# Two row buffers: taken from a pool for each batch, or made once and kept

## The chip, the cores and the metric

The kernel runs on one core of one Trainium2 chip. The metric is device time in microseconds for one execution; lower is better. Engines: TensorE (PE: matrix multiply, with PEld for its weight loads), VectorE (DVE), ScalarE (ACT), GpSimd (POOL) and SyncE (SP, which here issues most DMAs).

## The reference

Three parts follow one another, all in float32. `x` has 8 batches of 3072 tokens with 256 features.

1. The real part of a two-dimensional FFT of each batch (along tokens, then along features).
2. A mixture of 8 experts: every one of the 24,576 tokens is normalised, compared with 8 expert embeddings, sent to the best expert alone, and weighted by its softmax probability: `out[mask] = gate_w[mask, None] * (relu(x[mask] @ w1[e]) @ w2[e])`.
3. A gated layer on the result: `((x @ w_a) * (x @ w_b)) @ w_out`.

## The kernel before

The kernel has three stages that follow one another in one program: the batch stage (the transforms and the routing), the expert stage (groups of 256 tokens, sorted by expert), and the gated layer. In the trace the batch stage fills about the first 400 us. The program order of each engine is written out by hand (`manual_schedule`); nothing reorders it.

**One batch.** Batch `b` runs 8 steps `s1` (first half of the transform: 8 matmuls and 2 ScalarE copies each) and then 12 steps, `t` = 0 to 11. Each such step issues `s2(b, t)` (matmuls, one ScalarE copy `zs` at L378, two VectorE operations at L382) and then `s3(b, t - 2)`. `s3` makes two rows of 128 tokens: ScalarE copies one product out of PSUM (`qs`, L406), and VectorE writes row `t` (L407) and row 12 + `t` (L409) of the batch's row buffer `xo[b]`. So `s3(b, 0)` stands in the third step of the loop, and `s3(b, 10)` and `s3(b, 11)` stand in the first step of the next batch's `s1`. `post` then copies parts of the rows to their mirrored places (ScalarE, L421, for three values of `t` at a time).

**The row buffer.** `xo[b]` has 24 rows of 268 numbers on 128 partitions. There are two pools of one buffer each, `xo_p[0]` and `xo_p[1]`. Even batches take a tile from the first, odd batches from the second, at `t == 0` of `s3` (L389). The second pool is also used once at the start, as `spare` (L283), for small constants. A tile that is taken anew from a pool may be written when everything that used the pool's tile before it is over.

**Routing and scatters.** When a batch's rows are there, `route` (a chain of small VectorE operations, fed in between the other work by `advance`) finds the place of each token. Its last step (L557) makes `posi`, and then puts 24 scatters in `pool_q`: for `t` = 0 to 11, row `t` and row 12 + `t`. A scatter (L164) is an indirect DMA that GpSimd issues; it carries one row of 128 tokens from `xo[b]` to the sorted array `xs` in HBM. `drain(pool_q, ...)` issues one or two of them with each ScalarE copy that `mark` names, and `scatter` makes the scatter wait for that copy. The last ones of batch 6 are issued in one go behind the loop (L1024). In the program the scatters of batch `b` thus stand among the `s2` steps of batch `b + 1` and the `s1` steps of batch `b + 2`, whose rows go to the same buffer as those of `b`. GpSimd also does two of the folds of `x` for each batch (L257, `fold_v`).

**The end of the stage.** `p1b.close()` (L1026) gives back the pools on the right side, `xo_p[0]` among them, and the tiles of the expert stage (`slots[1]`, first written at L746) take their place. Rows of batch 7 stay in the other pool and are scattered during the expert stage.

Of the kernel before, what the change touches and what calls it, by code (L numbers as in the profile page):

```python
# [8 lines left out]
F32 = mybir.dt.float32  # L9
# [14 lines left out]
NT = 12  # L24
SEG = 67
ROW = 4 * SEG - 1
# [111 lines left out]
def moe_kernel(ctx, tc, x, emb, tau, w1, w2, wa, wb, wo, pa, pt, pr, nat, out):  # L138
# [44 lines left out]
    def scatter(idx_ap, src):  # L183
        i = spread(idx_ap, src, xs, NROWS - 1, "xs")
        if marks:
# [11 lines left out]
    xo_p = [p1b.enter_context(tc.tile_pool(name="xo0", bufs=1, side="right")),  # L197
            p1.enter_context(tc.tile_pool(name="xo1", bufs=1, side="left"))]
# [81 lines left out]
        return y  # L280


    spare = xo_p[1].tile([128, 2 * NT, ROW + 1], F32, name="xo").rearrange("p j c -> p (j c)")  # L283
    pcs = spare[:, 0:640]
    embt = spare[0:8, 640:896]
    su = ExitStack()
# [58 lines left out]
    xo = {}  # L345
# [40 lines left out]
    def s3(b, t):  # L386
        za, zb = zt.pop((b, t))
        if t == 0:
            xo[b] = xo_p[b % 2].tile([128, 2 * NT, ROW + 1], F32, name="xo")  # L389
            ssq[b] = r_p.tile([128, 2, NT], F32, name="ss", bufs=2)  # L390
        o = xo[b]
        ps = ps3.tile([128, 3, 137], F32, name="ps3")
        for i in range(2):
            q = 2 * t + i
            pe.matmul(ps[64 * i:64 * i + 64, 1, :], lhsT=tq(q), rhs=zb[:, i, :], start=True, stop=True)
        for i in range(2):
            q = 2 * t + i
            pe.matmul(ps[64 * i:64 * i + 64, 0, :], lhsT=tp(q), rhs=za[:, i, :], start=True, stop=True)
        pi = 0
        if t == 11:  # L400
            pi = 2
            for i in range(2):
                pe.matmul(ps[64 * i:64 * i + 64, 2, :], lhsT=tp2 if i else tp(22), rhs=za[:, i, :],
                          start=True, stop=True)
        qs = z_p.tile([128, 137], F32, name="qs")
        sc.copy(qs, ps[:, 1, :])  # L406
        ve.tensor_tensor(o[:, t, MAIN:MAIN + NCOL], ps[:, 0, :], qs, ALU.subtract)  # L407
        advance()
        ve.tensor_tensor(o[:, NT + t, MAIN:MAIN + NCOL], ps[:, pi, :], qs, ALU.add)  # L409
        advance()  # L410
# [157 lines left out]
    def advance(n=1):  # L568
        for _ in range(n):
            if routes:  # L570
                for g in list(routes):
                    r = next(g, 0)
                    if r == 0:
                        routes.remove(g)
                    if r != 1:
                        break
# [377 lines left out]
    for b in range(B):  # L954
# [3 lines left out]
        for s in range(8):  # L958
# [15 lines left out]
            if s == 0:  # L974
                s3(b - 1, 10)
                s3(b - 1, 11)
                post(b - 1, 9, 12)
                act_q.append(lambda b=b - 1, c=CHUNKS.get(b - 1, ((0, NT),))[-1]: start_route(b, *c))
# [23 lines left out]
        for t in range(NT + (2 if last else 0)):  # L1002
            if t < NT:
                s2(b, t)
            if t >= 2:
                s3(b, t - 2)
            if t in (5, 8, 11):
                post(b, t - 5, t - 2)
            if t == NT + 1:
                break  # L1010
            if t - 1 in chunks:
                act_q.append(lambda b=b, c=chunks[t - 1]: start_route(b, *c))
            if t % 3:
                drain(dve_q, 1)
            drain(act_q, 2)
            if last:
                advance(1)
                if t == 6:
                    weigh(0)
                if t == 8:  # L1020
                    turn(0)
# [237 lines left out]
    for st in range(NST):  # L1259
        G, p = divmod(st, NP)  # L1260
# [60 lines left out]
```

## Time and profile before

| | us |
|---|---|
| median of 3 runs (lowest, highest) | 3882.5 (3882.05, 3883.97) |
| the profiled execution's own time | 3879.51 |
| its span | 3877.7 |
| mean granted TensorE clock, share of full speed | 0.985 |

| engine | busy us | share of the span |
|---|---|---|
| PE | 3773.7 | 97% |
| DVE | 3121.0 | 80% |
| ACT | 1702.1 | 44% |
| POOL | 1136.6 | 29% |

The span is the time from the first to the last instruction of the profiled execution; its own time is 1.8 us more. Busy shares are means over three unlike stages. A stretch shows how busy each engine was between two times and which share of full speed TensorE's clock was granted (1.00 is 2.4 GHz, 0.50 is 1.2 GHz). In the lists in order of time a row is: start, duration, engine, line, operation, output and inputs, and in brackets how long the engine had been idle and what ended it; `issue` there means that no wait is seen. `DMA xs<-xo,posi` as a releaser is a scatter that has landed.

### The profile page before, as it was taken

Reading aid. Unit: us, or ns where it says so; the run is one execution under the profiler, and the core shown is the slowest. Engines: PE = TensorE matmul, PEld = TensorE weight load, DVE = VectorE, ACT = ScalarE, POOL = GpSimd, SP = SyncE. Lnnn points to the kernel's source line nnn. Section 1 sums busy time; section 2 is a strip of 40 time slices with the busy share of each in tenths; the row PEclk is TensorE's granted clock in tenths of the full one; section 3 lists DMA queues with packets and bytes.
Section 4 is the critical chain, followed back from the end, with each engine's and each line's share of the span. In section 5 each row is a group of like instructions: output and inputs, shape, how many; then the busy total and the mean of one; then the engine's idle time right before and its main releaser. Section 6 shows DMA issues by size and latency. Waiting matters only on the chain.

```text
span 3877.7 us, 68085 instructions
## 1 busy us (share of the span) xinstructions
PE 3773.7 (97%) x25556; PEld 3445.0 (89%) x25556; DVE 3121.0 (80%) x5097; ACT 1702.1 (44%) x3025; POOL 1136.6 (29%) x1017
## 2 busy tenths in 40 slices
PE   9888899999999999999999999999999999999998
PEld 8777899999999999888888888888888888888887
DVE  6766889899989987777788877788777788777886
ACT  4555566666666666433333333333333333333332
POOL 2666566667676643000000000000000000011011
PEclk8889899999999999999999999999999999999999
DMA  5444354333243231334334434444344344344331
GB/s 147 137 136 147 109 169 139 119 120 116 80 122 118 74 98 51 123 136 142 139 136 144 138 137 145 147 138 144 136 139 143 136 141 141 136 141 145 137 134 56
DMA packets 255048, 497.84 MB, mean 128 GB/s; under 512 B 151541, under 2 KB 184061, under 8 KB 245885
## 3 DMA queue, kind: packets, MB, share of 16 engines
q1 hardware_dynamic: 236284, 442.04, 35.1%
q0 software_dynamic: 18432, 51.44, 3.7%
q8 instruction: 201, 3.29, 0.3%
q14 instruction: 131, 1.07, 0.1%
HBM read 568.14 MB, written 95.14 MB: 171 GB/s over the span
## 4 chain that ended last, share of the span: by engine, by line
PE 59%; issue 18%; DVE 11%; POOL 2%; ACT 1%; DMA 0%; SPq 0%; POOLq 0%; ACTq 0%; DVEq 0%
PE pp L1142 7%; PE pp L1144 6%; PE pp L1143 6%; PE psy L819 5%; PE psy L820 5%; PE psy L821 5%; PE psh L794 5%; PE psh L790 5%; PE psh L792 4%; PE po L1212 3%; PE po L1210 3%; PE po L1211 3%; DVE big L1183 2%; DVE big L1168 2%; DVE gl L1194 1%
## 5 line engine op out<-in xcount | busy, mean ns | idle before, releaser
L164 POOL DMA_INDIRECT out_dram<-o,ig x192 | 215.3, 1121 | 2080.2 <-ACT o L1216 2033.5
L1189 ACT CAST gh<-big 128x512 fp32r<-128x512 f32 x576 | 355.8, 622 | 778.0 <-DVE big L1183 778.0
L1212 PE MATMUL po<-wo,gl 128*128 128x256 f32 x2304 | 651.1, 283 | 0.2 <-DVE gl L1194 0.2
L1210 PE MATMUL po<-wo,gh 128*128 128x256 f32 x2304 | 649.2, 282 | 1.6 <-ACT gh L1189 1.6
L1211 PE MATMUL po<-wo,gh 128*128 128x256 f32 x2304 | 647.4, 281 | 0.0
L747 DVE TENSOR_TENSOR s<-big,s 128x1024 fp32r<-128x1024 f32 x412 | 559.2, 1358 | 63.6 <-ACT s L746 62.2
L1142 PE MATMUL pp<-xo,slab 128*128 128x512 f32 x1440 | 582.8, 405 | 12.7 <-DVE big L1168 12.1
L1144 PE MATMUL pp<-xo,slab 128*128 128x512 f32 x1440 | 569.9, 396 | 0.0
L1143 PE MATMUL pp<-xo,slab 128*128 128x512 f32 x1440 | 566.7, 394 | 0.2 <-DVE xo L1126 0.2
L1211 PEld LDWEIGHTS po<-wo,gh 128*128 128x128 f32 x2304 | 435.5, 189 | 89.4
L1210 PEld LDWEIGHTS po<-wo,gh 128*128 128x128 f32 x2304 | 433.7, 188 | 88.9 <-ACT gh L1189 1.8
L819 PE MATMUL psy<-hh,s 128*128 128x256 f32 x1648 | 468.7, 284 | 13.5 <-ACT hh L802 13.5
L820 PE MATMUL psy<-hl,s 128*128 128x256 f32 x1648 | 468.4, 284 | 0.5 <-DVE hl L803 0.5
L821 PE MATMUL psy<-hh,s 128*128 128x256 f32 x1648 | 467.9, 284 | 0.0
L790 PE MATMUL psh<-xh,s 128*128 128x256 f32 x1648 | 452.9, 283 | 1.3 <-ACT xh L773 1.2
L794 PE MATMUL psh<-xh,s 128*128 128x256 f32 x1648 | 452.3, 283 | 0.0
L746 ACT CAST s<-big 128x1024 fp32r<-128x1024 f32 x412 | 428.8, 1041 | 16.4 <-DMA xs<-xo,posi 16.4
L1212 PEld LDWEIGHTS po<-wo,gl 128*128 128x128 f32 x2304 | 434.9, 189 | 0.4 <-DVE gl L1194 0.4
L1160 ACT COPY big<-pp 128x512 f32<-128x512 f32 x288 | 169.0, 587 | 584.7 <-PE pp L1144 581.9
L802 ACT ACTIVATE hh<-psh 128x512 fp32r<-128x512 f32 x412 | 246.4, 598 | 402.0 <-PE psh L794 271.1
L1194 DVE TENSOR_TENSOR gl<-big,gh 128x512 fp32r<-128x512 f32 x576 | 393.2, 683 | 2.9 <-ACT gh L1189 0.7
L1162 DVE TENSOR_TENSOR big<-pp,big 128x512 f32<-128x512 f32 x288 | 198.2, 688 | 238.2 <-PE pp L1144 209.5
(200 smaller groups left out, 8608.5 us busy)
## 6 DMA issues: line engine op xcount, KB each, us to landing
slab<-slabs SPq DMA_DIRECT2D x282, 896.0 KB
big<-in_w_dram SPq DMA_DIRECT2D x206, 1024.0 KB
big<-xs SPq DMA_DIRECT2D x103, 264.0 KB
ytd<-big SPq DMA_DIRECT2D x103, 256.0 KB
xr<-in_x_dram SPq DMA_DIRECT2D x32, 768.0 KB
big<-ytd SPq DMA_DIRECT2D x24, 1024.0 KB
slabs<-slab SPq DMA_DIRECT2D x12, 896.0 KB
xs<-xo,posi POOLq DMA_INDIRECT x192, 3.2
```

The lines of the kernel that those rows point to most:

```text
L747: ve.tensor_tensor(lo, r, hi.bitcast(F32), ALU.subtract)
L790: pe.matmul(ps[:, i, :], lhsT=wh, rhs=hi[:, k, :], start=(k == 0 and (u > 0 or i == 0)), stop=False, skip_group_check=True)
L794: pe.matmul(ps[:, i, :], lhsT=wl, rhs=hi[:, k, :], start=False, stop=last_, skip_group_check=True)
L819: pe.matmul(ps[:, c, :], lhsT=wh, rhs=a[:, i, :], start=st, stop=False, skip_group_check=True)
L820: pe.matmul(ps[:, c, :], lhsT=wh, rhs=l[:, i, :], start=False, stop=False, skip_group_check=True)
L821: pe.matmul(ps[:, c, :], lhsT=wl, rhs=a[:, i, :], start=False, stop=(f == 7), skip_group_check=True)
L1142: pe.matmul(ps, lhsT=t[:, wh, :], rhs=xh, start=start, stop=False, skip_group_check=True)
L1143: pe.matmul(ps, lhsT=t[:, wh, :], rhs=xl, start=False, stop=False, skip_group_check=True)
L1144: pe.matmul(ps, lhsT=t[:, wl, :], rhs=xh, start=False, stop=True, skip_group_check=True)
L1210: pe.matmul(ps, lhsT=ht, rhs=wos[0][:, f, :], start=(first_ and r % 2 == 0), stop=False, skip_group_check=True)
L1211: pe.matmul(ps, lhsT=ht, rhs=wos[1][:, f, :], start=False, stop=False, skip_group_check=True)
L1212: pe.matmul(ps, lhsT=lt, rhs=wos[0][:, f, :], start=False, stop=last_, skip_group_check=True)
```

## The change

The two row buffers are made once, before the loops, as the list `xos`. `s3` at `t == 0` no longer takes a tile: it names the one of the two that the batch uses. Buffers, sizes, places and all instructions stay as they are; lines behind the edit move by one.

```diff
-    spare = xo_p[1].tile([128, 2 * NT, ROW + 1], F32, name="xo").rearrange("p j c -> p (j c)")
+    xos = [p.tile([128, 2 * NT, ROW + 1], F32, name="xo") for p in xo_p]
+    spare = xos[1].rearrange("p j c -> p (j c)")
...
         if t == 0:
-            xo[b] = xo_p[b % 2].tile([128, 2 * NT, ROW + 1], F32, name="xo")
+            xo[b] = xos[b % 2]
```

The instructions of every engine stand in the same order before and after. What differs is which semaphores some of them wait for. This is VectorE at `s3(2, 0)` and `s3(2, 1)`, the first rows that are written to a used buffer; the instructions between are the routing of batch 1 (L538 to L549), a fold (L257) and `s2` (L382). `DMASW0` to `DMASW7` are the eight semaphores that the scatters count up in turn. Before:

```order
L407 TENSOR_TENSOR xo<-ps_1303,qs 128x137 [waits DMASW4_49,DMASW3_49,DMASW5_49,DMASW2_49,DMASW6_49,DMASW1_49,DMASW7_49,DMASW0_49,Activation_49]
L538 COPY xo<-natt 128x24
L409 TENSOR_TENSOR xo<-ps_1303,qs 128x137
L540 RECIPROCAL mx<-mx 128x24 [waits DVE_49]
L257 TENSOR_TENSOR big_71<-xr 96x4x127
L382 SCALAR_TENSOR_TENSOR zc<-sgnx,psb,psa 128x137 [waits PE_49,Activation_49]
L543 COPY xo<-mx 128x48 [waits DVE_49]
L543 COPY xo<-mx 128x48
L382 SCALAR_TENSOR_TENSOR zc<-sgnx,psb,psa 128x137
L547 TENSOR_TENSOR pref<-ps_122,prt 128x8
L407 TENSOR_TENSOR xo<-ps_1330,qs 128x137 [waits Activation_49]
L549 TENSOR_TENSOR inc<-inc,pref 128x192 [waits DVE_49]
```

And now, with all line numbers one higher:

```order
L408 TENSOR_TENSOR xo<-ps_1301,qs 128x137 [waits DMASW0_49,Activation_49]
L539 COPY xo<-natt 128x24
L410 TENSOR_TENSOR xo<-ps_1301,qs 128x137 [waits DMASW1_49]
L541 RECIPROCAL mx<-mx 128x24 [waits DVE_49]
L257 TENSOR_TENSOR big_71<-xr 96x4x127
L383 SCALAR_TENSOR_TENSOR zc<-sgnx,psb,psa 128x137 [waits PE_49,Activation_49]
L544 COPY xo<-mx 128x48 [waits DVE_49]
L544 COPY xo<-mx 128x48
L383 SCALAR_TENSOR_TENSOR zc<-sgnx,psb,psa 128x137
L548 TENSOR_TENSOR pref<-ps_122,prt 128x8
L408 TENSOR_TENSOR xo<-ps_1328,qs 128x137 [waits DMASW2_49,Activation_49]
L550 TENSOR_TENSOR inc<-inc,pref 128x192 [waits DVE_49]
```

The first L407 of the batch waited for all eight scatter semaphores and the others for none. Now each L407 and each L409 waits for one, that of the scatter that last read its row. This is so in each of batches 2 to 7: of the 96 L407, 6 had nine waits and 90 one; now 72 have two and 24 one, and 72 of the 96 L409 have one where none had any. On ScalarE the first L421 of each of these batches had nine waits; now 23 of L421 have seven (six scatter semaphores and VectorE's). On GpSimd one scatter waits for two loads into `spare` besides. Nothing else differs.

## Rows read from the trace of the kernel before

**Rows 1.** Waits, 0 to 1100 us: who waits for whom; us, times, longest

```profile
DVE xo L407 <- DMA xs<-xo,posi: 48.2, 6, 8.9
PE ps L395 <- DVE xo L409: 37.9, 6, 7.3
ACT s L746 <- DMA xs<-xo,posi: 16.4, 1, 16.4
```

**Rows 2.** VectorE in time order, L407 at t = 0

```profile
83.80 0.29 DVE L407 TENSOR_TENSOR xo<-ps,qs 128x137 f32<-128x137 f32 x1
129.71 0.30 DVE L407 TENSOR_TENSOR xo<-ps,qs 128x137 f32<-128x137 f32 x1 [8.75 <-DMA xs<-xo,posi]
176.71 0.30 DVE L407 TENSOR_TENSOR xo<-ps,qs 128x137 f32<-128x137 f32 x1 [8.76 <-DMA xs<-xo,posi]
319.67 0.30 DVE L407 TENSOR_TENSOR xo<-ps,qs 128x137 f32<-128x137 f32 x1 [8.02 <-DMA xs<-xo,posi]
364.70 0.30 DVE L407 TENSOR_TENSOR xo<-ps,qs 128x137 f32<-128x137 f32 x1 [4.99 <-DMA xs<-xo,posi]
```

**Rows 3.** VectorE in time order, L407 at t = 10, batches 1, 2, 6

```profile
101.97 0.30 DVE L407 TENSOR_TENSOR xo<-ps,qs 128x137 f32<-128x137 f32 x1 [2.21 <-ACT qs L406]
148.96 0.30 DVE L407 TENSOR_TENSOR xo<-ps,qs 128x137 f32<-128x137 f32 x1 [2.21 <-ACT qs L406]
339.50 0.30 DVE L407 TENSOR_TENSOR xo<-ps,qs 128x137 f32<-128x137 f32 x1 [2.06 <-ACT qs L406]
```

**Rows 4.** Stretches: length, busy us of PE, PEld, DVE, ACT, POOL, granted clock, DMA

```profile
84.00:90.00 6.00, 6.00 (x59) 4.79 (x57) 6.00 (x26) 3.11 (x10) 1.03 (x1) 1.00 0.36 93
224.00:230.00 6.00, 4.89 (x26) 3.91 (x27) 5.22 (x23) 1.05 (x5) 0.90 (x1) 0.50 0.46 120
```

**Rows 5.** GpSimd in time order, scatters of the steady batches

```profile
100.75 0.97 POOL L164 DMA_INDIRECT xs<-xo,posi  x1 [1.26 <-ACT yt L360]
127.13 0.97 POOL L164 DMA_INDIRECT xs<-xo,posi  x1 [0.30 <-issue]
134.72 0.97 POOL L164 DMA_INDIRECT xs<-xo,posi  x1 [6.61 <-issue]
210.90 1.14 POOL L164 DMA_INDIRECT xs<-xo,posi  x1 [0.30 <-issue]
212.35 1.21 POOL L164 DMA_INDIRECT xs<-xo,posi  x1 [0.31 <-issue]
```

**Rows 6.** GpSimd in time order, the last scatters of the batch stage

```profile
341.55 0.97 POOL L164 DMA_INDIRECT xs<-xo,posi  x1 [1.02 <-ACT yt L360]
369.71 0.97 POOL L164 DMA_INDIRECT xs<-xo,posi  x1 [1.27 <-ACT zs L378]
374.69 0.99 POOL L164 DMA_INDIRECT xs<-xo,posi  x1 [0.63 <-ACT zs L378]
384.62 0.97 POOL L164 DMA_INDIRECT xs<-xo,posi  x1 [0.30 <-issue]
397.39 0.97 POOL L164 DMA_INDIRECT xs<-xo,posi  x1 [0.31 <-DMA xs<-xo,posi]
```

**Rows 7.** ScalarE, then TensorE, in time order, where the expert stage starts

```profile
400.03 1.04 ACT L746 CAST s<-big 128x1024 fp32r<-128x1024 f32 x1 [16.37 <-DMA xs<-xo,posi]
402.01 0.58 PE L819 MATMUL psy<-hh,s 128*128 128x256 f32 x1 [13.49 <-ACT hh L802]
```

**Rows 8.** Lines L164, L407, L421: operation, count, ns min/median/max, first and last

```profile
L164 POOL DMA_INDIRECT xs<-xo,posi x192: 967/973/1932, 89.0 to 529.2; - x192
L407 DVEq EVENT_SEMAPHORE  x24: 49/50/50, 126.0 to 364.6; - x24
L421 ACTq EVENT_SEMAPHORE  x24: 38/38/38, 135.3 to 368.1; - x24
```

**Rows 9.** Waits for and of the loads of x: the queue's own, then GpSimd's

```profile
SPq L241 <- DVE big L257: 184.3, 14, 19.9
POOL big L257 <- DMA xr<-in_x_dram: 52.0, 5, 20.3
```

## The prediction

> **What bounds the kernel now.** I read three views. First the list of waits: VectorE's L407, the write of a row, waits for scatters 48.2 us in 6 waits, and TensorE waits 37.9 us for VectorE's next write L409 in the same 6 places [rows 1]. Then VectorE in order of time: the waits stand at `t` = 0 of batches 2 to 7, the first rows that go into a used buffer. Batch 1, which has no scatter to wait for, starts its row 0 at 83.80 without any wait [rows 2]. Then GpSimd in order of time: the last scatter of batch 0 is issued at 127.13, and VectorE's L407 of batch 2 starts at 129.71, when it has landed, 2.58 us later [rows 2, 5]. So VectorE stands still with GpSimd's backlog, although row 0 and row 12 of that buffer were sent 22 scatters earlier. Nobody gains by that wait: GpSimd is idle for 6.61 us behind it until the next batch's routing, which VectorE does, is done [rows 5].
>
> What the stage's end hangs on is a second question. The expert stage starts when ScalarE's L746 may write where batch 6's buffer was; it waits 16.4 us for scatters and starts at 400.03, 2.64 us behind the issue of the last one at 397.39, and TensorE, idle for 13.49 us, goes on at 402.01 [rows 1, 6, 7]. So a shorter batch loop pays only as far as GpSimd's last scatter comes earlier. Everything behind 400 us is the same program with the same order and the same waits, with TensorE nearly always busy; I take it to move as one block.
>
> **The change part by part.** No instruction is added, removed or moved. In batches 2 to 7 the one wait for all 24 scatters becomes a wait per row.
>
> *The wait that goes.* Its size at `t` = 0 is 48.2 us [rows 1]. What is late next: the other inputs of L407 are there when its idle time begins, so it can start then, at 129.71 - 8.75 = 120.96 in batch 2. The new waits do not bind if the scatters stay as far ahead as they are. Measured from 120.96, the last scatter starts at +6.2 and has landed at +8.8, and two scatters (2 x 1.277 us, as 384.62 to 397.39 is ten of them [rows 6]) belong to each `t`. Row 0's pair has therefore landed at 8.8 - 11 x 2.55 = -19, and row 11's at +8.8, while VectorE comes to row 11 behind row 10, which it reaches 18.17 us after row 0 in batch 1 (101.97 - 83.80) [rows 2, 3]. The smallest margin is some 9 us, in row 11.
>
> *The cold start that goes with it.* Behind each wait TensorE's clock is at 0.50 (1.2 GHz) for some 6 us, where batch 1 in the same place has 1.00 (2.4 GHz) [rows 4]. Batch 1 reaches row 10 after 18.17 us, batch 2 after 148.96 - 129.71 = 19.25, batch 6 after 339.50 - 319.67 = 19.83 [rows 2, 3]. Over the five batches 2 to 6 the excess is 1.08 to 2.04 us, 7.9 in all. Bounds: 0 to 7.9 us. I take all of it, since batch 1 is a batch of the new kind, run in this trace: its whole cycle, to where batch 2 could have started, is 120.96 - 83.80 = 37.16 us, against 47.00 for the next (176.71 - 129.71).
>
> *Whether GpSimd follows.* A batch without any idle time costs it 7 x 1.277 us for seven scatters, then 27.35 us from the eighth (issued at 100.75, when the first copy of `s1` is done) to the end of the last with the two folds between, and 0.30: 36.6 us [rows 5]. That is just under the 37.16. So it keeps pace, with the eighth scatter of each batch still waiting for its copy, as in batch 1; the margin is half a microsecond.
>
> *The end, in GpSimd's time.* Batch 6's row 0 moves from 319.67 by 48.2 - 5.0 = 43.2 (the five waits up to it) and by 7.9 - 1.7 = 6.2 to 270.2. The tenth scatter of batch 5, at 341.55, stood 21.9 behind it; without the cold start 20.2, so it comes at 290.4. From there 20 more scatters at 1.277 lead to the sixth of batch 6: 316.0 (in the trace it is at 369.71, held up by the last wait). From the sixth to the seventh are 4.98 us (a GpSimd copy between them waits until the sixth has landed), and from the seventh to the end of the last 397.39 + 0.97 - 374.69 = 23.67 [rows 6]. The end comes at 344.7, against 398.36: 53.7 us. With nothing won from the clock the same sum ends at 352.6: 45.8 us. With a GpSimd that is never idle behind batch 0 (128.4 + 4 x 36.6 + 29 x 1.277 + 4.98 + 23.67 = 340.5) it is 57.9; more is not to be had.
>
> *What the new waits cost.* Nine waits were four extra semaphore instructions (24 for six L407), so a second wait is one of them, at 50 ns [rows 8]: 72 instead of 24 on VectorE, 2.4 us in all. VectorE is full only in the first 6 us of the loop (6.00 of 6.00 in batch 1 [rows 4]), which is three rows of a batch; I count 0.2 us for each of five batches, between 0 and 0.4. ScalarE gets 69 instead of 24 at 38 ns, 1.7 us in all, beside 3.11 us of work in 6.00 [rows 4, 8]: hidden; if it were not, 0.3 us for a batch.
>
> *Scatters beside VectorE.* The last five scatters of each batch now run while VectorE does the routing, no longer while it stands still. The trace has such company at 210.90 and 212.35, where routing ran: 1.14 and 1.21 us instead of 0.97 [rows 5], 0.4 us for a batch. Bounds: 0, and 0.96 each (the longest of the 192 took 1.93 [rows 8]), 4.8 us for a batch. I take 0.4, the rows nearest in kind, for five batches. The Trainium skill ("SBUF — State Buffer", section "Who interferes with whom") says that VectorE and GpSimd share a port pair under an exclusive lock, and that a copy on VectorE in a two-port mode keeps GpSimd from writing descriptors until it ends. By that rule the upper bound is near; the two rows speak for the lower one.
>
> Sum: 53.7 - 5 x 0.2 - 5 x 0.4 = 50.7 us. The profiled execution took 3879.5, so 3828.8; the median of the runs stands 3.0 above that execution, so 3831.8.
>
> **The rivals.**
>
> *GpSimd becomes the bound (faster, but by less).* With 4.8 us more for each batch its cycle is 41.4, above 37.16, and it is never idle again: 128.4 + 4 x 41.4 + 29 x 1.277 + 4.8 + 4.98 + 23.67 = 364.5, so 33.9 us are won: 3848.6. For it: the margin of half a microsecond, and the rule of the page above. Against it: the median scatter is at 0.973, next to the minimum of 0.967 [rows 8].
>
> *The loads of x set the pace, and the gain is hidden.* Then the batch keeps its 47 us and the time stays at 3882.5. Against it: the queue of the loads waits 184.3 us for VectorE's folds, so it is the loads that are held back; loads that GpSimd waited for (52.0 us, 5 times) are those of the start [rows 9].
>
> *Slower: the waits by row bind.* If GpSimd fell behind by more than the 9 us of row 11, VectorE would wait in row after row, and since each scatter also waits for a ScalarE copy that waits for VectorE, the three would go in step: two scatters and a landing for each row, 2 x 1.277 + 2.58 = 5.1 us instead of 1.8 (18.17 over ten rows), 40 us more for a batch. Over six batches that is 238 us, less the 48.2 that go: 4072. Against it: GpSimd catches up in each batch as long as its 36.6 us are not much above the cycle, and a slower VectorE gives it more time, so the lag should settle short of that point.
>
> That the change does not do what it says can be left out: the eight-fold wait is gone from the program.
>
> **How the numbers follow.** The forecast has 0.84, GpSimd as the bound 0.09, the loads 0.03, the waits by row 0.02; 0.02 is left for what I do not see. The forecast's own range goes from the idle-free GpSimd (57.9: 3824.6) to no gain from the clock with the costs taken (45.8 - 3.0 = 42.8: 3839.7). I widen it to 3822 to 3844, which takes in some of the first rival. About 0.2% (8 us) can be told from no change. Faster by more: 0.94 (the forecast, the first rival, and half of the rest); within: 0.03; slower: 0.03.
>
> **What would show it.** Right: no waits of L407 for scatters; row 0 to row 0 in about 37 to 38 us; granted clock 1.00 through batches 2 to 6; GpSimd issuing with few pauses above 0.30; L746 at about 349 us, after a wait for scatters somewhat longer than before (18 to 20 us), as the loop moves a little more than GpSimd. Wrong: scatters well above 1 us in the first 6 us of a batch (first rival), VectorE or GpSimd waiting for loads of x behind 100 us (second), waits of L407 or L409 for scatters at `t` above 0 (third), or a later stage that gives the time back.

## The result

The changed kernel takes 3828.0 us (median of 4 runs, 3825.3 to 3830.4) where the kernel before took 3883.2 beside it: a ratio of 0.986, 95% interval 0.9847 to 0.9873. The forecast was 3831.8 us. A second measurement gave 3828.5 against 3881.2, 0.9873 (0.9857 to 0.989). The profiled executions, on which the sum was made, stand at 3879.51 before and 3827.76 after: 51.75 us, where the sum had 50.7. The forecast then added 3.0 us, by which the median before stood above its profiled execution; the new median stands only 0.3 above its own, which makes 2.7 of the 3.8 us between forecast and result.

The line numbers behind the change are one higher: L408 and L410 are the two row writes L407 and L409, L747 is L746, L820 is L819.

The waits of the first 1100 us (who waits for whom; us in total, times, longest), against [rows 1]:

```profile
ACT qs L407 <- PE ps L399: 42.5, 76, 1.2
...
ACT s L747 <- DMA xs<-xo,posi: 16.4, 1, 16.4
...
PE psy L820 <- ACT hh L803: 13.5, 1, 13.5
```

The 48.2 us of VectorE and the 37.9 us of TensorE in [rows 1] have no line any more. ScalarE's one wait for the last scatter of batch 6, and TensorE's behind it, are as long as they were. VectorE in order of time, row write at `t` = 0 of batches 1 to 7, against [rows 2]:

```profile
84.09 0.29 DVE L408 TENSOR_TENSOR xo<-ps,qs 128x137 f32<-128x137 f32 x1
121.17 0.28 DVE L408 TENSOR_TENSOR xo<-ps,qs 128x137 f32<-128x137 f32 x1
158.42 0.29 DVE L408 TENSOR_TENSOR xo<-ps,qs 128x137 f32<-128x137 f32 x1
195.67 0.29 DVE L408 TENSOR_TENSOR xo<-ps,qs 128x137 f32<-128x137 f32 x1
232.97 0.29 DVE L408 TENSOR_TENSOR xo<-ps,qs 128x137 f32<-128x137 f32 x1
271.16 0.33 DVE L408 TENSOR_TENSOR xo<-ps,qs 128x137 f32<-128x137 f32 x1
309.98 0.30 DVE L408 TENSOR_TENSOR xo<-ps,qs 128x137 f32<-128x137 f32 x1 [0.23 <-ACT qs L407]
```

From row 0 to row 0 it is now 37.08, 37.25, 37.25 and 37.30 us, then 38.2 and 38.8 in the batches that carry more routing; it was 47.00 from 129.71 to 176.71. Behind row 0 the clock is no longer at half (stretches, columns as in [rows 4]):

```profile
195.00:201.00 6.00, 6.00 (x57) 4.90 (x54) 5.99 (x28) 2.54 (x9) 4.48 (x6) 1.00 0.40 127
233.00:239.00 6.00, 6.00 (x56) 4.97 (x54) 6.00 (x31) 2.74 (x9) 4.77 (x5) 1.00 0.53 150
```

These are batches 4 and 5, the first from 0.7 us ahead of row 0, the second from row 0 on. In [rows 4] the same place of batch 4 has 0.50 and TensorE busy for 4.89 of 6 us. GpSimd in order of time, the places of [rows 5, 6]: the last scatter of batch 0, the tenth of batch 5, the sixth and seventh of batch 6 with the copy between them, and the end:

```profile
127.49 0.97 POOL L164 DMA_INDIRECT xs<-xo,posi  x1 [0.30 <-ACT xo L422]
...
291.60 0.97 POOL L164 DMA_INDIRECT xs<-xo,posi  x1 [1.03 <-ACT yt L361]
...
317.21 0.97 POOL L164 DMA_INDIRECT xs<-xo,posi  x1 [0.30 <-issue]
321.74 0.19 POOL L758 COPY big<-big 32x8 int32<-32x8 int32 x1 [3.56 <-DMA xs<-xo,posi]
322.56 0.98 POOL L164 DMA_INDIRECT xs<-xo,posi  x1 [0.63 <-ACT qs L407]
...
344.88 0.97 POOL L164 DMA_INDIRECT xs<-xo,posi  x1 [0.30 <-DMA xs<-xo,posi]
```

The last scatter ends at 345.85, where the costless sum had 344.7 and the sum with its costs 347.7. What follows it, ScalarE and then TensorE in order of time, against [rows 7]:

```profile
347.51 1.04 ACT L747 CAST s<-big 128x1024 fp32r<-128x1024 f32 x1 [16.36 <-DMA xs<-xo,posi]
```

```profile
349.50 0.58 PE L820 MATMUL psy<-hh,s 128*128 128x256 f32 x1 [13.49 <-ACT hh L803]
```

ScalarE starts 52.52 us earlier than at 400.03, TensorE 52.51 earlier than at 402.01. From the end of the last scatter to the end of the program it was 3877.7 - 398.36 = 3479.3 us before and is 3825.9 - 345.85 = 3480.1 now: the rest moved as one block, but for 0.7 us that it gave back.

### The profile page after: what moved, and what is told of

Its sections match the earlier page's. It is cut to its first block, busy times and chain, and to the rows that moved or that the text cites. A ratio compares the mean times of both kernels' runs of the same rounds, so it can differ in the third digit from the quotient of the medians.

```text
span 3825.9 us, 68179 instructions
## 1 busy us (share of the span) xinstructions
PE 3758.0 (98%) x25556; PEld 3431.9 (90%) x25556; DVE 3119.0 (82%) x5097; ACT 1701.9 (44%) x3025; POOL 1138.9 (30%) x1017
## 4 chain that ended last, share of the span: by engine, by line
PE 62%; issue 19%; DVE 12%; POOL 3%; ACT 2%; DMA 1%; SPq 0%; POOLq 0%; ACTq 0%; DVEq 0%
PE pp L1143 7%; PE pp L1145 6%; PE pp L1144 6%; PE psy L820 4%; PE psy L821 4%; PE psy L822 4%; PE psh L795 4%; PE psh L791 4%; PE po L1213 4%; PE po L1211 4%; PE po L1212 3%; PE psh L793 3%; DVE big L1184 2%; DVE big L1169 2%; PE ps L357 2%
## 5 line engine op out<-in xcount | busy, mean ns | idle before, releaser
L164 POOL DMA_INDIRECT out_dram<-o,ig x192 | 215.2, 1121 | 2080.6 <-ACT o L1217 2033.9
L748 DVE TENSOR_TENSOR s<-big,s 128x1024 fp32r<-128x1024 f32 x412 | 560.3, 1360 | 63.6 <-ACT s L747 61.5
L820 PE MATMUL psy<-hh,s 128*128 128x256 f32 x1648 | 468.1, 284 | 13.5 <-ACT hh L803 13.5
L747 ACT CAST s<-big 128x1024 fp32r<-128x1024 f32 x412 | 428.9, 1041 | 16.4 <-DMA xs<-xo,posi 16.4
```

Of the source, the lines that this page charges most:

```text
L748: ve.tensor_tensor(lo, r, hi.bitcast(F32), ALU.subtract)
L820: pe.matmul(ps[:, c, :], lhsT=wh, rhs=a[:, i, :], start=st, stop=False, skip_group_check=True)
```

## Experiments

Five questions were put to the chip. Six runs, in two sets in which several of these kernels were measured together, are inconclusive; they are told last. The runs told first are of one kernel alone beside the kernel before. Differences between two of these kernels are taken across such pairs, in which the kernel before took 3879.5 to 3883.2 us, and are good to a few us; the traces are finer.

**Half of the change: only the odd batches' buffer is kept.**

```
-    xos = [p.tile([128, 2 * NT, ROW + 1], F32, name="xo") for p in xo_p]
+    xos = [None, xo_p[1].tile([128, 2 * NT, ROW + 1], F32, name="xo")]
...
-            xo[b] = xos[b % 2]
+            xo[b] = xos[1] if b % 2 else xo_p[0].tile([128, 2 * NT, ROW + 1], F32, name="xo")
```

> The kernel with only the buffer of the odd batches kept, unaltered, alone beside the kernel before. Where it was run earlier the kernel before took 3893 and 3906 us, and all engines had unexplained idle times of 4 to 7 us in each batch; where the changed kernel was run the kernel before took 3881 to 3883. If the kernel before takes 3881 to 3883 here and those idle times are absent: 3853 to 3861 us by the theory (the waits of batches 3, 5 and 7, 22.7 us, and half of the cold start go, the others stay), 3873 to 3883 by the rival (what is taken away in an odd batch comes back in the even batch behind it). If the idle times belong to this kernel, it takes about as long as the kernel before although that is at 3882.

Measured: 3856.9 us against 3879.9, ratio 0.9943 (0.9927 to 0.996): 22.9 us faster, the profiled execution 24.2 faster than that of the kernel before. VectorE's row write in order of time:

```profile
130.13 0.30 DVE L408 TENSOR_TENSOR xo<-ps,qs 128x137 f32<-128x137 f32 x1 [8.79 <-DMA xs<-xo,posi]
...
214.88 0.30 DVE L408 TENSOR_TENSOR xo<-ps,qs 128x137 f32<-128x137 f32 x1 [8.74 <-DMA xs<-xo,posi]
...
299.10 0.30 DVE L408 TENSOR_TENSOR xo<-ps,qs 128x137 f32<-128x137 f32 x1 [8.28 <-DMA xs<-xo,posi]
```

These are batches 2, 4 and 6, and they are all: 25.8 us in 3 waits. The waits of batches 2 and 4 are as long as they were (8.75 and 8.74), that of batch 6 is 0.26 us longer (8.02). From row 0 of batch 2 to that of batch 3 are 38.67 us (130.13 to 168.80), from 3 to 4 46.08. So the waits are separate costs: what is taken away in one batch does not come back in the next. The time lies inside the theory's 3853 to 3861 and far from the rival's 3873.

**The cold start alone: the waits stay, TensorE is kept at work in them.**

```
+        if t == 2 and b > 1:
+            fill = corner()
+            for _ in range({6: 20, 7: 10}.get(b, 24)):
+                pe.matmul(fill, lhsT=ones, rhs=ones, start=True, stop=True)
+            uses[1] += 1
```

> The kernel before with its pool and waits, and dummy multiplications of ones on TensorE in the 6 to 7 us of each batch in which it stood idle, unaltered, alone beside the kernel before (in the earlier set all kernels had stalls). Theory (the cold start is a term of its own): VectorE waits 48 us for the scatters as before, the granted clock of 6 us behind the wait of batch 4 is 1.00 and no longer 0.50, and the time is 5 to 8 us below the kernel before. Rival (the slow multiplications lie beside the next wait, which takes their time up, since each batch's wait ends with a scatter that GpSimd starts from its own chain): the clock rises, the waits grow by as much, the time stays within 1.5 us.

Measured: 3875.7 us against 3881.0, ratio 0.9985 (0.9976 to 0.9994), 5.3 us with an interval from 2 to 9. VectorE waits 47.9 us in 6 waits, as long as before, so the rival falls. Stretches of 6 us about the end of the waits of batches 2 to 5 (columns as in [rows 4]):

```profile
130.00:136.00 6.00, 4.17 (x28) 3.35 (x29) 5.68 (x25) 1.53 (x6) 0.67 (x1) 0.77 0.48 128
177.00:183.00 6.00, 3.96 (x38) 3.28 (x40) 5.78 (x25) 2.15 (x7) 0.77 (x1) 1.00 0.50 126
223.00:229.00 6.00, 4.57 (x29) 3.76 (x30) 5.60 (x25) 1.52 (x6) 0.97 (x1) 0.72 0.51 132
270.00:276.00 6.00, 4.41 (x42) 3.62 (x42) 5.91 (x29) 2.20 (x7) 0.90 (x1) 1.00 0.53 130
```

The clock held in batches 3 and 5 and fell in part in 2, 4 and 6 (0.63 from 316 to 322), where the expectation for batch 4 is missed; why every second one is open. It makes a comparison inside one execution. VectorE's row 0 of batches 2 to 6:

```profile
130.32 0.30 DVE L412 TENSOR_TENSOR xo<-ps,qs 128x137 f32<-128x137 f32 x1 [8.89 <-DMA xs<-xo,posi]
177.22 0.30 DVE L412 TENSOR_TENSOR xo<-ps,qs 128x137 f32<-128x137 f32 x1 [8.75 <-DMA xs<-xo,posi]
222.91 0.30 DVE L412 TENSOR_TENSOR xo<-ps,qs 128x137 f32<-128x137 f32 x1 [8.78 <-DMA xs<-xo,posi]
270.09 0.30 DVE L412 TENSOR_TENSOR xo<-ps,qs 128x137 f32<-128x137 f32 x1 [9.02 <-DMA xs<-xo,posi]
315.98 0.30 DVE L412 TENSOR_TENSOR xo<-ps,qs 128x137 f32<-128x137 f32 x1 [8.06 <-DMA xs<-xo,posi]
```

The batches with the clock held take 45.69 and 45.89 us, batches 2 and 4 46.90 and 47.18. Batches 3 to 5 of the kernel before, beside [rows 2], where the waits of batches 4 and 5 are not shown:

```profile
224.08 0.30 DVE L407 TENSOR_TENSOR xo<-ps,qs 128x137 f32<-128x137 f32 x1 [8.74 <-DMA xs<-xo,posi]
271.84 0.30 DVE L407 TENSOR_TENSOR xo<-ps,qs 128x137 f32<-128x137 f32 x1 [8.92 <-DMA xs<-xo,posi]
```

There batch 3 takes 47.37 us (from 176.71) and batch 5 47.83 (from 271.84). By this a cold start costs 1.7 and 1.9 us of a batch, and 1.2 to 1.3 beside batches 2 and 4 of the same execution, which were cold in part. All four lie inside the prediction's excess of 1.08 to 2.04 us, and the clock is a term of its own.

**Six scatters more at the end of batch 6.** The last six row blocks are written again, into a scratch table that nobody reads.

```
+    xs2 = dram.tile([NROWS, ROW], F32, name="xs2")
...
+    for k in range(6):
+        spread(*rows[(B - 1) * 2 * NT - 6 + k], xs2, NROWS - 1, "xs2")
```

> The kernel with six more scatters behind batch 6, unaltered, alone beside the kernel before, since alone the kernel with the odd buffer kept showed none of the stalls and took 3856.9 us with the kernel before at 3879.9. Theory (the last scatter on GpSimd releases the expert stage): the changed kernel's 3828.5 us and 6 x 1.28 = 7.7 more, 3835 to 3838 where the kernel before takes 3880 to 3882, and ScalarE's wait for the scatters ahead of the first weight split of group 1 grows from 16.4 to about 24 us. Rival (VectorE and TensorE set the start of the expert stage): 3828 to 3830, the wait unchanged at its end.

Measured: 3836.7 us against 3882.1, ratio 0.9882 (0.9865 to 0.9898): 8.3 us above the changed kernel's 3828.5, taken on another chip. ScalarE in order of time:

```profile
355.14 1.04 ACT L750 CAST s<-big 128x1024 fp32r<-128x1024 f32 x1 [24.18 <-DMA xs<-xo,posi]
```

That is 7.63 us behind 347.51, after a wait of 24.2 us, as six scatters at 1.28 ask for. GpSimd's last scatter sets the start of the expert stage; the rival had 0 to 2 us.

**Four scatters more in each of batches 1 to 4**, again into a scratch table.

```
+        b, k = divmod(len(scatters) - 1, 2 * NT)
+        if b in (1, 2, 3, 4) and k >= 2 * NT - 4:
+            spread(idx_ap, src, xs2, NROWS - 1, "xs2")
```

> The changed kernel with four more scatters in each of batches 1 to 4 (the last four row blocks of each a second time, into a scratch table that nobody reads), unaltered, alone beside the kernel before (in the earlier set all kernels had stalls): 16 x 1.28 = 20.4 us more on GpSimd. Theory (GpSimd has 0.6 to 0.9 us free in a batch of 37.2 us, so 3 to 5 us over batches 2 to 6, and sets the end): +14 to +18 us against 3828.5, 3842 to 3847, the scatters of each batch ending later by some 4 us than those of the one before it did, and no wait for scatters at the row subtraction in batches 2 to 4. Rival (TensorE and VectorE set the pace, GpSimd may run late by up to the 9 us margin of the rows and catches up behind batch 5): 0 to +5 us. Second rival (the rows' own waits bind as soon as GpSimd falls behind): +20 us or more, with waits for scatters at the row subtraction in most batches.

Measured: 3846.6 us against 3879.5, ratio 0.9913 (0.99 to 0.9927): 18.1 us above 3828.5, and ScalarE's split behind the last scatter starts at 365.70, 18.2 later. The row write never waits for a scatter, so the second rival falls, and the first had at most 5. The sum is the theory's, just above its 14 to 18; the way there is not quite. From row 0 to row 0 it is 41.4, 40.5, 42.7 and 41.2 us from batch 3 on, near GpSimd's new time of 36.6 + 4 x 1.28 = 41.7, with VectorE at work or waiting for ScalarE. VectorE, then GpSimd, ahead of row 0 of batches 4, 5 and 6:

```profile
188.27 0.18 DVE L278 TENSOR_TENSOR rt<-ry,rh 128x24 f32<-128x24 f32 x1
188.49 3.03 DVE L280 TENSOR_TENSOR rt<-rt,ry 128x24 f32<-128x24 f32 x1
...
230.64 2.39 DVE L271 TENSOR_SCALAR rt<-ss 128x24 int32<-128x24 int32 x1 [1.31 <-ACT junk L421]
...
272.75 2.94 DVE L278 TENSOR_TENSOR rt<-ry,rh 128x24 f32<-128x24 f32 x1
```

```profile
189.11 2.36 POOL L261 TENSOR_TENSOR big<-xr 96x1016 f32<-96x1016 f32 x1
...
230.63 2.36 POOL L261 TENSOR_TENSOR big<-xr 96x1016 f32<-96x1016 f32 x1
...
273.28 2.37 POOL L261 TENSOR_TENSOR big<-xr 96x1016 f32<-96x1016 f32 x1
```

An operation of the routing on 24 columns, 0.18 us elsewhere, lasts 3.03, 2.39 and 2.94 us, each time to within 0.05 us of the end of a fold that GpSimd runs late: GpSimd's lateness reaches VectorE's routing, and through it TensorE, without any wait on a semaphore. TensorE, idle for 0.7 us at this point of batch 3 in the changed kernel, is idle for 3.2, 2.5 and 3.5 us. Behind the first and the third of these gaps the granted clock is for most of 6 us at 1.2 GHz, 0.56 and 0.55 on average (stretches, columns as in [rows 4]):

```profile
196.00:202.00 6.00, 5.16 (x25) 4.81 (x26) 4.61 (x18) 0.77 (x3) 4.48 (x5) 0.56 0.42 141
278.00:284.00 6.00, 3.98 (x21) 3.62 (x21) 4.85 (x16) 1.03 (x3) 4.47 (x6) 0.55 0.82 326
```

Batches 3 and 5, which end in them, are the two longest. GpSimd itself is never idle for more than 0.31 us from 141 to 339 us, so the end is still its sum, as the theory had it. In batch 6 (41.2 us) no such operation is found, and what lengthens it was not shown.

**A version that goes on: work beside the last scatters.** In the expert stage a group of tokens goes through up steps (the product with `w1`), whose result behind the ReLU is `hh`, and down steps (`hh` with `w2`). A split makes two parts of a weight: a copy in the type fp32r (ScalarE, L747) and what that leaves over (VectorE, L748).

```
-    slots[1] = [[sl1_p.tile(..., name=f"s1{w}{i}") for i in range(2)] for w in range(2)]
+    slots[1][::-1] = [[sl1_p.tile(..., name=f"s1{w}{i}") for i in range(2)] for w in (1, 0)]
...
-            split_w(g + 1, u)
+            if g or u < 2:
+                split_w(g + 1, u)
+            elif u == 3:
+                split_w(1, 2)
+                split_w(1, 3)
...
-            (gp if g else ve)      # in weigh and halves
+            (gp if g > 1 else ve)
```

> The changed kernel with three edits behind batch 6: the four weight slots of group 1 change places in memory, so that those of the up weights no longer lie over the kept buffer of the even batches; the split of group 1's down weights comes behind the last up step of group 0; weighing and splitting the rows of group 1 is done on VectorE, not behind the scatters on GpSimd. Theory (ScalarE's 16.4 us wait for the last scatter of batch 6 and the 13.5 us in which TensorE then stands idle are what is left of the stage's end): the down steps of group 0 and the up steps of group 1 run beside the last scatters, TensorE's idle time falls from 13.5 to 3 to 5 us, and the time by 8 to 11 us, to 3817 to 3821. Rival (something else is late there: the weights of group 1, or the rows of the second half, which wait for batch 7's scatters on GpSimd): the wait moves a few instructions on, 0 to -3 us.

Measured: 3822.1 us against 3881.8, ratio 0.985 (0.9836 to 0.9863): some 6 us below the changed kernel by the medians, between the theory's 8 to 11 and the rival's 3. The two were not measured side by side, and this interval overlaps with the changed kernel's (0.9847 to 0.9873), so that the time alone does not show it to be the faster one. TensorE, ScalarE and GpSimd in order of time:

```profile
352.41 0.58 PE L820 MATMUL psy<-hh,s 128*128 128x256 f32 x1 [6.40 <-ACT hh L803]
```

```profile
349.45 1.99 ACT L747 CAST s<-big 128x1024 fp32r<-128x1024 f32 x2 [10.46 <-DMA xs<-xo,posi]
```

```profile
330.27 2.00 POOL L164 DMA_INDIRECT xs<-xo,posi  x1 [0.30 <-DVE xl L775]
332.57 1.43 POOL L164 DMA_INDIRECT xs<-xo,posi  x1 [0.30 <-issue]
334.31 1.43 POOL L164 DMA_INDIRECT xs<-xo,posi  x1 [0.30 <-issue]
336.04 1.51 POOL L164 DMA_INDIRECT xs<-xo,posi  x1 [0.30 <-issue]
...
346.82 0.98 POOL L164 DMA_INDIRECT xs<-xo,posi  x1 [0.30 <-issue]
```

Two things in these rows stand against the rest of the gain. The split that was put later still waits for the last scatter, and `hh` of group 1 stands behind it on ScalarE, so TensorE is idle for 6.40 us, not 3 to 5. And the last scatter comes at 346.82, 1.94 later: four scatters took 6.4 us instead of the usual 3.9 while VectorE did the added work. Next would be to move that split behind the first `hh` of group 1; it was not tried.

**The inconclusive sets.** Four of these kernels were first measured in one set, two of them later in another. What was expected of them:

> The kernel before with half of the change: the row buffer of the odd batches is kept, that of the even ones is still taken anew from its pool. Theory: the six waits of the row subtraction are separate costs. The waits of batches 3, 5 and 7 (8.8 + 8.9 + 5.0 = 22.7 us) go, those of batches 2, 4 and 6 stay at 8 to 9 us each, and half of the cold start of TensorE goes too (about 3.5 us): about -26 us against the kernel before, 3853 to 3861. Rival: the scatters of one batch must end somewhere, so that the wait removed in an odd batch comes back in the even batch behind it, which then waits 15 us or more: 0 to -8 us.

> The kernel before with its pool and its waits as they were, and dummy multiplications of ones put on TensorE ahead of the multiplications of row tile 2 in batches 2 to 7 (24 in batches 2 to 5, 20 in batch 6, 10 in batch 7, each two records of about 0.14 us), so that TensorE works in the 6 to 7 us in which it stood idle. Theory (the cold start is a term of its own in the gain): VectorE still waits 48 us for the scatters, the granted clock of the stretch 6 to 12 us behind each wait rises from 0.50 to 1.00, the cycle of a batch falls from 47 us to about 45.7, and the time by 5 to 8 us, to 3875 to 3878. Rival (the slow matmuls behind a wait lie beside the next wait, which takes their time up): the clock rises, the waits grow by as much, the time stays within 1 us of 3883.

> The changed kernel with six more scatters behind the last one of batch 6: the last six row blocks are written a second time, into a scratch table that nobody reads. Theory (the last scatter on GpSimd is what releases the expert stage): 6 x 1.28 = 7.7 us later, 3834.5 to 3837. Rival (the expert stage's start is set by VectorE and TensorE, which end their row tiles at about the same time): 0 to 2 us.

> The changed kernel with four more scatters in each of batches 1 to 4 (the last four row blocks of each a second time, into a scratch table that nobody reads): 16 x 1.28 = 20.4 us more on GpSimd. Theory (GpSimd has about 0.6 us free in a batch of 37.2 us, 3 to 5 us over batches 2 to 6, and sets the end): +14 to +18 us, 3842 to 3846, with waits for GpSimd's folds or rows still hidden. Rival (TensorE and VectorE set the pace and GpSimd can run later by up to the 9 us margin of the rows and catch up): 0 to +5 us. Second rival (the rows' own waits bind as soon as GpSimd falls behind, and hold VectorE in each batch): +20 us or more, with waits for scatters back at the row subtraction.

> The changed kernel itself once more, unaltered, as a control. In the kernel with six more scatters behind batch 6 the batches 2 to 5 took 47 us each although their instructions stand as in the changed kernel, which took 37.2, and TensorE, ScalarE and VectorE stood idle there for 4 to 7 us at a time with nothing named that released them. If that came from the chip or the run and not from the added scatters, this kernel is slow in the same way here: about 3893 us, 7.7 below that run's 3900.5, and no faster than the kernel before. If it came from the added scatters, it takes 3828 us again, 1.4% below the kernel before.

> The kernel with six more scatters behind batch 6, once more, unaltered: the changed kernel, run again, took 3828.5 us with the kernel before at 3881.2, and this one had taken 3900.5 with the kernel before at 3893.4. If the stalls of 4 to 7 us came with that earlier set of runs, this takes 3834 to 3838 us now (3828.5 + 7.7 by the theory, 3828.5 to 3830.5 by the rival in which VectorE and TensorE set the start of the expert stage). If the added scatters bring them, it takes about 3890 us again.

> The kernel with only the buffer of the odd batches kept, once more, unaltered. If the stalls came with the earlier set of runs: 3853 to 3861 us by the theory (the waits of batches 3, 5 and 7 go, those of 2, 4 and 6 stay), 3873 to 3883 by the rival (what is taken away in an odd batch comes back in the even batch behind it). If the kernel itself has them: about 3881 us, as the kernel before.

Measured in the first set, the kernel before at 3893.4 us: odd buffer kept 3893.5 (0.9998), warm 3913.1 (1.0052), six scatters 3900.5 (1.002), four scatters per batch 3913.2 (1.0053). In the second, the kernel before at 3906.3: six scatters 3913.5 (1.0021), odd buffer kept 3905.2 (0.9997). No theory's number is met; the odd buffer kept, at the time of the kernel before, would even suit its rival's 0 to -8 us. Between the two sets stood the changed kernel alone, at its 3828.5 us, and behind them the runs above. That control spoke for the added scatters, and the second set for the kernels themselves; the runs alone, of the same kernels unaltered, took both back. Six scatters more, in the first set, waits from 80 to 420 us:

```profile
ACT zs L382 <- remote: 26.6, 7, 5.3
PEld psb L381 <- issue: 24.5, 45, 3.7
...
ACT s L750 <- DMA xs<-xo,posi: 20.4, 1, 20.4
```

In the same kernel alone no line names `remote`. With it a batch takes 47.1 us from 84.17 to 131.30, alone 37.1 from 83.80 to 120.89, and behind the last scatter both need the same time within a few us. So something stops ScalarE, VectorE and TensorE for 3 to 7 us at a time in each batch, while GpSimd goes on with its scatters, and it comes with the set and not with the kernel: one of the four ran alone on the same chip as in the first set, and showed nothing of it. What it is stays open. The kernel before loses only 10 to 25 us by it. That its waits for scatters cover most of it is likely but not shown, as there is no trace of it from these sets; in the warm kernel, which has the same waits, VectorE's waits ahead of row 0 are 0 to 3.8 us there, where they are 4.4 to 9.0 alone. How the changed kernel itself does under it was not measured; with six scatters more it was 0.2% behind the kernel before.

## Why the prediction was right

*The wait that goes.* All 48.2 us went, and on VectorE no wait by row took their place (on ScalarE one of 0.26 us did, ahead of L422 at 163.80). Half of the change brought 22.9 us (24.2 in the profiled executions) of the 26 that its three waits and half the cold start make, which shows that the waits add up batch by batch; the 2 to 3 us that are missing stay open.

*The cold start.* Counted at its upper bound of 7.9 us, 6.2 of them up to row 0 of batch 6. The warm kernel, in three of whose five batches the clock still fell in part, gained 5.3. In the changed kernel, row 0 to row 0 less the wait at its end fell over batches 2 to 5 from 155.5 to 150.0 us: 5.5 us came, with the price of the new waits taken off, so the term was about right and a little high. The choice to take batch 1 as the model of the new batch (37.16) held within 0.15 us: 37.08 to 37.30 in batches 1 to 4.

*Whether GpSimd follows.* It does, with half a microsecond to spare as said: in batches 2 to 5 it is idle for 0.9 us, instead of the usual 0.30, at one scatter per batch or so, behind a copy of ScalarE's (1.03 at 291.60). The four extra scatters show the other side: there, from batch 3 on, it is never idle beyond the usual 0.30, and the loop takes about its time. So the first rival was no more than about half a microsecond per batch away, as a mechanism.

*The end, in GpSimd's time.* The step that carries the forecast: the six scatters behind batch 6 show directly that the last scatter sets it (+7.6 for 7.7). Its pieces: the tenth scatter of batch 5 at 290.4 was 291.60, the sixth of batch 6 at 316.0 was 317.21, the end at 344.7 was 345.85.

*The costs.* Here the term was mis-sized: 5 x 0.2 for the new semaphore waits and 5 x 0.4 for scatters beside VectorE, 3.0 us, of which at most 1.15 reached the end (345.85 against 344.7), and 0.29 of that were there at row 0 of batch 1 (84.09 against 83.80). Another 0.7 stand in the cycles of batches 2 to 5, by the new waits or by a cold start that was worth less. That the sum came within 1.1 us of the 51.75 is thus in part luck: a third of the counted costs arrived, and 0.7 us that it did not count were given back behind the scatters. The line of the new waits on VectorE, that of all scatters, to be set beside [rows 8], and two scatters that ran beside the routing:

```profile
L408 DVEq EVENT_SEMAPHORE  x72: 21/21/21, 120.0 to 327.9; - x72
```

```profile
L164 POOL DMA_INDIRECT xs<-xo,posi x192: 966/973/1996, 89.3 to 476.4; - x192
```

```profile
159.22 1.37 POOL L164 DMA_INDIRECT xs<-xo,posi  x1 [0.30 <-ACT zs L379]
...
271.80 1.55 POOL L164 DMA_INDIRECT xs<-xo,posi  x1 [0.31 <-issue]
```

The count of 72 was right, the price was 21 ns and not 50: 0.25 us for the twelve of a batch instead of 0.6. How much of it the cycle shows is open: batches 2 to 4 take 37.25 to 37.30 us, batch 1, which has none of these waits, 37.08. The last five scatters of a batch, which now run beside VectorE's routing, took 0.06, 0.41, 0.06, 0.34 and 0.58 us together beyond 0.97 each in batches 2 to 6: 1.4 us in all where 2.0 were counted, and far from the upper bound of 4.8 for each batch. The scatter of 2.00 us stands behind the batches, at 384.45; the median stayed at 0.973. So the lower bound was the nearer one, as the two rows in [rows 5] had said. The rule of the Trainium skill on the shared port ("SBUF — State Buffer", section "Who interferes with whom") that was weighed there did not make the upper bound come true here.

*What would show it.* All signs came but one, with row 0 to row 0 at 38.2 and 38.8 in the last two batches: ScalarE's wait at L747 was to grow to 18 to 20 us and stayed at 16.36, since the loop and GpSimd moved by the same 52.5 us.

*The other rivals.* Loads of x: the queue of the loads still waits for VectorE's folds (139.2 us, 184.3 before), and the batch lost its 10 us, so they set no pace. Waits by row: none on VectorE, even with four scatters more per batch.

## What to carry to other kernels

A tile that is taken anew from a pool waits for every reader of the whole old tile; a tile that is kept waits row by row, and where rows are read long before the last one this alone was 48 us here. Ask then which engine's last instruction releases the next stage, and make the sum in that engine's time: the gain is what that instruction moves, and it is shown at once by adding a few like it at the end. And look, behind each wait that goes, for what the clock did there: here it was 5.5 us in batches 2 to 5, a tenth of the gain.

## What the runs showed of the hardware

- The semaphore record that a second wait puts ahead of an instruction takes 21 ns on VectorE's queue (72 of 72 in the changed kernel, where the scatters had long landed), and 50 in the kernel before (24 of 24, ahead of a wait that held).
- An operation of VectorE with two operands in SBUF stood still until a GpSimd fold had ended: 3.03 us instead of 0.18, beside a fold of 2.36 (its record begins 0.62 us ahead of the fold's). The Trainium skill says so ("SBUF — State Buffer", section "Who interferes with whom": an instruction of VectorE with two inputs in SBUF contends with one of GpSimd that reads SBUF), and the rows agree. In the next batch a TENSOR_SCALAR with one such operand stood in the same way, for 2.39 us.
- Four scatters on GpSimd stretched from 0.97 to between 1.43 and 2.00 us while VectorE ran the splits of 128x1024 and the work moved to it in the last version, whose last scatter came 1.9 us later.
- 48 records of dummy multiplications, 5.5 us in all, ahead of a wait's end left the granted clock at 1.00 behind the wait in batches 3 and 5, and at 0.77 and 0.72 in batches 2 and 4, in the same order of instructions.
